# A fused retention and MLP kernel on one core: stores of short units as one stepped transfer, new constants in the emission planner, another order of loads and delays

## The chip, the cores and the metric

The kernel runs on one NeuronCore of a Trainium2 chip. The metric is the device time of one execution in microseconds; less is better. The core has TensorE (PE; its weight loads are shown apart as PEld), VectorE (DVE), ScalarE (ACT), GpSimd (POOL) and SyncE (SP), which run side by side and wait for each other by semaphores, and 16 DMA engines that all transfers share.

## The reference

Causal retention over 8 batches, 8 heads, 576 positions and a head size of 64, and behind it an MLP with an exact GELU:

```
scores = (q @ k^T) / sqrt(64)
gamma  = 1 - 2 ** (-5 - head)
ret    = scores * where(i >= j, gamma ** (i - j), 0)
x      = (ret @ v), heads side by side      # 4608 tokens x 512
out    = gelu_exact(x @ w_in) @ w_out       # 512 -> 2048 -> 512, float32
```

## The kernel before

**Units and blocks.** A batch of 576 positions is cut into chunks of 128; the last one has 64 (TAIL). A *unit* is one chunk of one batch, or, for the tails, the tails of two neighbouring batches together: 64 rows of one and 64 rows of the other, 128 partitions. These are the *short units* (the third entry of their tuple in `units` is None). There are 36 units. Four units make a *block* of 512 tokens for the MLP, nine blocks t = 0 to 8. Units 16 and 17 are short and open block 4; units 34 and 35 are short and are the last two of block 8, the last block.

**Retention.** Per unit or pair of units: loads of q, k and v (POOL's queue, L328, with a cast to bf16), a transpose of q and k (on TensorE for the first groups, L568, by a DMA transpose on SP's queue for the others, L578), scores (L602, L611, L621), the mask on DVE, the inner product with v (L684, L692, L710), the running state (L520, L729) and its product with q (L765). Most of these matmuls are 64 x 64 and use a part of TensorE's array; they are set as groups of 16 to 128 between the MLP's full matmuls.

**MLP.** w_in is applied by L812 (blocks 0 to 5) or by a seven-product Strassen scheme, L1079 (blocks 6 to 8); w_out by L857 (block 0) or by a seven-product scheme, L998. The products of the latter are called M1 to M7 and come in the order M3, M4, M5, M1, M2, M6, M7. For the last two units of a block (tile `hi`), M2 gives the left 256 columns of the output (a copy, L547), M6 the right 256 (L948); for the first two (tile `lo`), M5 and M7 do the same (L958 or L963). In the last block a result is stored as soon as it is there, in pieces.

**The order of the work.** The program is written out straight, without loops on the chip. A planner in the Python code (`fire`, `mlp_pick`, `cand`, the main loop at the end) keeps estimated times of each engine in `T`, of each transfer in two modelled queues (`transfer`, `run_queues`, the costs `MOVE`, the delays SW_LATE and HW_LATE) and of the fetching of TensorE's instructions (`fetch_of`: a block is used up after each 127.7 matmuls, the first after 95; BEGIN, BRING and USE are the times that a fetch takes). It always emits next what it thinks can begin first. Where `stall` says that a group of small matmuls would run into a block not yet fetched by more than STALL, the group is put off. So a changed constant changes no instruction, but which one comes when. `ORDER` is a list found by search: first the order of the loads on POOL's queue (`wi3` is a piece of w_in, `k4` the keys of unit 4, `io` the iota and what hangs on it, `dq2` a decay factor), then entries such as `s10+0.5`, `b24+0.5`, `z12+2.5`, `p29+34`, `u1+8` with delays for scores, inner products, DVE, MLP pieces and haste, and `a17`, units whose v is scaled on ACT instead of DVE.

**Stores.** `store` (L837) writes rows of a unit. A short unit's rows go to two batches; `rows_of` gives the two places, and `store` issues one transfer for each. SP's queue carries the stores and the DMA transposes, in the order of emission; a few stores of the last block go on ACT's queue. At the end of the last block, `after` (L927) does this behind M2 and M6:

```
if last and p == M2:                      # L972
    for x in range(2):
        if units[4 * t + 2 + x][2] is not None:
            store(t, 2 + x, hi[:, x, LEFT], 0, 256)
...
if last:                                  # behind M6, L950
    lo_col = 0 if units[4 * t + 2 + x][2] is None else 256
    store(t, 2 + x, hi[:, x, lo_col:], lo_col, 512, nc.scalar, nc.sync)
```

Both of these units are short, so nothing leaves after M2, and after M6 each unit leaves as two transfers of 64 rows by 512 columns, one on ACT's queue and one on SP's.

Of the kernel before, what the change touches and what calls it, by code (L numbers as in the profile page):

```python
# [17 lines left out]
def kernel(  # L18
# [14 lines left out]
    nc = tc.nc  # L33
    ctx.enter_context(tc.manual_schedule())

    B, H, S, D = q.shape
    d_model = H * D
# [4 lines left out]
    C = 128  # L42
# [5 lines left out]
    TAIL = S - (NCI - 1) * C  # L48
# [5 lines left out]
    units = [(bp, 0, j) for bp in range(2) for j in range(2)]  # L54
# [52 lines left out]
    T = dict.fromkeys(("pe", "act", "dve", "pool", "sp"), 0.0)  # L107
# [9 lines left out]
    for n, keys in enumerate(HW_FIRST):  # L117
        t = o_pool.tile([128, 2, H, D], FP32, tag=f"o{n}", name="first")
        for x, (what, i) in enumerate(keys):
            first[what, i] = t[:, x]  # L120
            src = {"q": q, "k": k, "v": v}[what][2 * units[i][0] + units[i][2]]
# [82 lines left out]
        nc.vector.tensor_tensor(s[:, 3:5], w[:, :, 0:256], w[:, :, 256:512], op=ALU.add)  # L204
        ws_at[i] = on("dve", 1.05, land_out[i]) + SEM

    SW_LATE, HW_LATE = 4.2, 2.8
    TURN_SHARES, STORE_SHARES = (0.455, 0.545), (0.455, 0.545)
    MOVE = {"wi": 1.33, "wo": 1.42, "ld": 0.89, "short": 0.44, "turn": 1.88, "store": 0.9}
    queues = ([], [])  # L210
    moved = [0.0, [0, 0], [None, None]]

# [49 lines left out]
    def sw_dma(issue, kind, put):  # L262
# [3 lines left out]
        T["pool"] += issue  # L266
        flying.append(transfer(0, at, MOVE[kind], put))

    def hw_dma(issue, work, ready, put=lambda end: None, shares=TURN_SHARES):
        at = max(T["sp"], ready)  # L270
        if len(hw_flying) >= 3:
            T["sp"] = max(T["sp"], hw_flying[-3]["end"])
        T["sp"] = max(T["sp"], at + issue)
        hw_flying.append(transfer(1, at, work, put, shares))

    def putter(where, key):
        def put(end):
            where[key] = end
        return put
# [55 lines left out]
    for x, keys in enumerate(zip(*HW_FIRST)):  # L335
        for n, (what, i) in enumerate(keys):
            land[what, i] = (4.6, 5.2)[n] + 0.75 * x
            t = tiles_of(i)
            cast_due[what, i] = (t[1] if what == "v" else t[0][:, "qk".index(what)], first[what, i])
    ORDER = ("wi0 k1 v2 io wi1 q1 v0 k2 v1 q2 wi2 k3 wi3 wi4 q3 wi6 wi5 wi7 v3 k4 wo0 q4 k5 q5 v5 v4 wo1 wo2 dq2 wo3 "  # L340
             "q6 wo4 k7 wo6 q7 dq3 dq0 k6 wo7 v6 v7 wo5 dq4 z12+2.5 p29+34 a17 a31 s10+0.5 z35+2 a30 a23 b24+0.5 s24+4 "
             "s17+0 p25+30 z32+0.2 a13 s12+4 a10 s35+5 s31+5 a27 s18+3 a24 s7+3 u1+8 b25+1.5 a8 p21+36 p27+28 p26+34 "
             "b4+0.8 z27+2 a9 a11 z23+0.2 a25 a26 a5 z4+2.5 b32+4 p35+28 p28+28 a21 b22+3 a15 b17+2 b35+0.5 p30+34 "
             "z16+0.4 z20+1.2 z13+0.8 s14+5 s28+1.5 b30+4 b28+0.5 b8+0.3 s32+5 s29+0.5 z11+0.6 b23+0.5 b12+1.5 p22+30 "
             "b7+4 z34+0.2 s19+5 p20+32 s5+2 z18+0.6 u4+0 b21+0.8 z14+1.2 z26+0.6 b19+0.3 b13+3 s30+1 b20+1 p32+30 "
             "s16+3 b11+4 z33+0.2 b26+0.8 u6+12 z10+0.2 z6+2.5 b5+2 a16 s21+3 z22+0.6 b27+3 z28+2.5 p31+34 u7+12 "
             "b16+1.5 z19+1.2 u3+20 s13+3 s26+5 b9+2 s23+3 s4+1 b33+0.5 z29+0.2 b14+1.5 b18+0.3 z5+1.5 a14 b10+1.5 "
             "b34+0.5 u2+28 s25+0.5 z25+1.5 s34+5 s15+4 s6+3").split()

    BY_ACT = {int(x[1:]) for x in ORDER if x[0] == "a"}  # L350
    S_LATE = {int(x[1:].split("+")[0]): float(x.split("+")[1]) for x in ORDER if x[0] == "s"}
    B_LATE = {int(x[1:].split("+")[0]): float(x.split("+")[1]) for x in ORDER if x[0] == "b"}
    DVE_LAG, P_WAIT, HURRY = ({int(x[1:].split("+")[0]): float(x.split("+")[1]) for x in ORDER if x[0] == kind} for kind in "zpu")
    ORDER = [x for x in ORDER if x[0] not in "abszpu"]

    rest = const.tile([128, 2], BF16, name="rest")

    for n, g in enumerate(groups):
        ORDER += [what + str(i) for what in "qkv" for i in g if what + str(i) not in ORDER and (what, i) not in first]

# [73 lines left out]
    SEM = 0.12  # L434

    CHUNK, FIRST_CHUNK, ASKED = 127.7, 95.0, 150.0
    BEGIN, BEGIN_IDLE, BRING, USE = 4.8, 1.4, 1.2, 1.5
    fetched = {"count": N_WARM, "next": FIRST_CHUNK, "ask": FIRST_CHUNK + CHUNK - ASKED, "ready": [0.0], "landed": 0.0}

    def fetch_of(f, now, dur, n):  # L440
# [133 lines left out]
    def turn_dma(n, jj):  # L574
# [9 lines left out]

        hw_dma(1.3, MOVE["turn"] * (0.62 if short else 1.0), max(land["qk"[jj], i] for i in groups[n]), put)

# [244 lines left out]
    def rows_of(t, ts):  # L831
        bp, ci, j = units[t * 4 + ts]
        if j is not None:
            return [((2 * bp + j) * S + ci * C, 0, C)]
        return [((2 * bp + jj) * S + ci * C, TAIL * jj, TAIL) for jj in range(2)]

    def store(t, ts, src, lo=0, hi=d_model, *on_queues):  # L837
        for x, (row, p0, n) in enumerate(rows_of(t, ts)):
            queue = on_queues[x] if on_queues else nc.sync
            queue.dma_start(out[row:row + n, lo:hi], src[p0:p0 + n])  # L840
        for _ in rows_of(t, ts):
            hw_dma(0.4, MOVE["store"] * (hi - lo) / d_model / len(rows_of(t, ts)), max(T["act"], T["dve"]), putter(o_free, (t, ts // 2)), STORE_SHARES)

    def o_tile(t, x):
        if t == N_BLK - 2:
# [31 lines left out]
    o_free = {}  # L877
# [3 lines left out]
    LEFT, RIGHT = slice(0, 256), slice(256, 512)  # L881
# [45 lines left out]
    def after(t, p, done, piece):  # L927
        lo, hi = o_tiles[t, 0], o_tiles[t, 1]
        last = t == N_BLK - 1
        b, m = held_bank[t, bank_of[p], piece if last and p == M7 else 0]  # L930
        if p == M3:
            nc.scalar.copy(hi[:, :, RIGHT], m)
            at = on("act", 0.6, max(done, o_at(t, 1)))
        elif p == M4:
            for n, (xs, c0, c1) in enumerate(pieces(t)):
                z = held_bank[t, "Z", n] = seeded([128, xs.stop - xs.start, c1 - c0], "m")
                nc.vector.tensor_tensor(z[1], hi[:, xs, 256 + c0:256 + c1], m[:, xs, c0:c1], op=ALU.add)
                at = on("dve", 0.15 + 0.00104 * (xs.stop - xs.start) * (c1 - c0), max(done, read_at[t, M3]))
        elif p == M1:
            v = held_bank[t, "V", 0] = seeded([128, 2, 256], "m")  # L940
            for n, (xs, c0, c1) in enumerate(pieces(t)):
                at = either(0.42 if last else 0.68, done, v[1][:, xs, c0:c1], held_bank[t, "Z", n][1], -1.0)
        elif p in (M5, M2):
            at = either(0.68, max(done, o_at(t, p == M2)), lo[:, :, RIGHT] if p == M5 else hi[:, :, LEFT], m)
            release(b, at + SEM)
        elif p == M6:
            for x in (1, 0) if last else (slice(0, 2),):
                nc.vector.scalar_tensor_tensor(hi[:, x, RIGHT], m[:, x], -1.0, hi[:, x, LEFT], op0=ALU.mult, op1=MINUS)  # L948
                at = on("dve", 0.42 if last else 0.68, max(done, read_at[t, M2]))
                if last:  # L950
                    lo_col = 0 if units[4 * t + 2 + x][2] is None else 256
                    store(t, 2 + x, hi[:, x, lo_col:], lo_col, 512, nc.scalar, nc.sync)
            release(b, at + SEM)
            for x in range(2 * (not last)):
                store(t, 2 + x, hi[:, x, :])
        elif last:
            x, c0, c1 = PIECES[piece]
            nc.vector.tensor_tensor(lo[:, x, c0:c1], m[:, 0], lo[:, x, 256 + c0:256 + c1], op=MINUS)  # L958
            at = on("dve", 0.15 + 0.00104 * (c1 - c0), done)
            release(b, at + SEM)  # L960
            store(t, x, lo[:, x, c0:c1], c0, c1, nc.scalar if piece == 1 else nc.sync)
        else:
            nc.vector.tensor_tensor(lo[:, :, LEFT], m, lo[:, :, RIGHT], op=MINUS)  # L963
            at = on("dve", 0.68, max(done, read_at[t, M5]))
            release(b, at + SEM)
            for x in range(2):
                for c0, c1 in ((0, 256), (256, 512)) if t == N_BLK - 2 else ((0, 512),):
                    store(t, x, lo[:, x, c0:c1], c0, c1)
        if last and p == M5:
            for x in range(2):  # L970
                store(t, x, lo[:, x, RIGHT], 256, 512)
        if last and p == M2:  # L972
            for x in range(2):
                if units[4 * t + 2 + x][2] is not None:
                    store(t, 2 + x, hi[:, x, LEFT], 0, 256)
        read_at[t, p] = at + SEM

    def pieces(t):
# [323 lines left out]
        pe(0.2158 * n, n)  # L1302
        release(b, T["pe"])

    STALL = 0.05

    rest_of = []
    AFTER = [(0.437, 4)] * 6
# [58 lines left out]
    b, t = bank([128, 512], FP32, "warm")  # L1367
# [4 lines left out]
    while True:  # L1372
# [22 lines left out]
        if nA < N_U and not rest_of:  # L1395
            n = group_of[nA]
# [3 lines left out]
        if nB < nA and not rest_of:  # L1400
# [5 lines left out]
            n = group_of[back[0]]  # L1406
# [9 lines left out]
            if not hurry and first:  # L1416
                kind, t = first[0], first[1]
                hurry = nB < 4 * t + 4 if kind in "14" else len(runs[0]) <= HURRY.get(t, 8 if t + 1 >= FAST else 16) and nB < 4 * t + 8 + 4 * (t + 1 >= FAST)
            if hurry:
                n = out_banks(back) + starts(back) + 2 * bool(g)  # L1420
                along = not early and nA >= 4 and scored <= now and len(frees(n)) == n and free_time(n) <= now + 0.3
                cand(ready, "S", g if along else [], back)
        if g and scored < 1e8:
            if early or stuck:
                cand(max(scored, free_time(2)) if nA - nB <= 2 else 1e9, "S", g, [])
            else:
# [4 lines left out]
                if free and (not back or back_at <= now + 0.3) and nA + len(g) <= ahead:  # L1431
                    n = 2 + out_banks(back) + starts(back)
# [13 lines left out]
        if due:  # L1446
            _, kind, a = due[0]
            if kind == "X":
                n = group_of[nX]
# [75 lines left out]
```

## Time and profile before

| | |
|---|---|
| median of 3 runs | 288.71 us (288.49 to 289.89) |
| the profiled execution, its own time | 288.38 us |
| its span, first to last instruction | 286.5 us, TensorE's granted clock 0.998 |
| busy: PE, DVE, ACT, POOL | 276.8, 194.1, 161.2, 115.2 us |
| last arithmetic ends | 281.41 us after the span's start |

The profile shows one execution. Times in it are counted from the span's start. A line of the timeline has start, duration, engine, source line, operation, output and inputs, shape and count, and in brackets the time that the engine was idle just before with what ended it ("issue" means that nothing in the profile ended it). SPq and ACTq are the queues that issue transfers; the duration is that of the issue, the landing comes later. A DMA view has the busy share of the 16 DMA engines in 40 equal slices of its window, in tenths, and the packets of each queue with the time that they took as a share of 16 engines over the window.

### The profile page before, as it was taken

The page shows a single profiled execution, that of the slowest core. Times are in us where ns is not written, and L with a number is a line of the kernel's source. Part 1 is how long each engine was busy: PE and PEld are TensorE (multiplying, and loading weights), DVE is VectorE, ACT ScalarE, POOL GpSimd, SP SyncE. Part 2 cuts the span into 40 slices and gives each one's busy share as a digit, 9 for nine tenths or more (in the row PEclk, how much of TensorE's full clock was granted, in tenths as well). Part 3 has the DMA queues.
Part 4 walks back from the last instruction along what each step waited for, and adds up shares of the span by engine and source line. Part 5 has one row for each costly group of instructions (what it writes and reads, how often), then busy time and mean ns, then how long its engine had stood idle before and what let it go on. Part 6 is the DMA issues. An engine that isn't in the chain of part 4 may idle for free.

```text
span 286.5 us, 9550 instructions
## 1 busy us (share of the span) xinstructions
PE 276.8 (97%) x4076; PEld 207.1 (72%) x4076; DVE 194.1 (68%) x400; ACT 161.2 (56%) x384; POOL 115.2 (40%) x144
## 2 busy tenths in 40 slices
PE   8999999999999999999999999999999999999992
PEld 3588767587865488548864686468888788888892
DVE  4663788628464694999555914994699978869722
ACT  5567835896377911865668338643566445455320
POOL 8978999963555373428462364200000000000000
PEclk9999999999999999999999999999999999999999
DMA  9999999999999999999999999970040000300223
GB/s 141 169 187 172 189 178 163 154 127 160 191 152 218 139 129 138 237 128 145 142 187 186 120 149 158 210 77 2 2 149 2 2 1 19 132 1 2 102 83 111
DMA packets 152507, 35.49 MB, mean 124 GB/s; under 512 B 141072, under 2 KB 148368, under 8 KB 152464
## 3 DMA queue, kind: packets, MB, share of 16 engines
q0 software_dynamic: 116832, 18.10, 97.0%
q1 hardware_dynamic: 34288, 16.19, 33.5%
q10 hardware_dynamic: 1344, 0.59, 0.8%
q8 instruction: 32, 0.52, 0.8%
q14 instruction: 11, 0.09, 0.2%
HBM read 36.70 MB, written 9.44 MB: 161 GB/s over the span
## 4 chain that ended last, share of the span: by engine, by line
PE 73%; POOL 12%; DMA 9%; DVE 1%; issue 1%; SPq 1%; POOLq 0%; DVEq 0%
PE m L998 34%; PE hT L812 21%; PE f L1079 13%; DMA qkT<-qk_ld 4%; DMA w_in<-in_moe_w_in_dram 3%; POOL qk_ld L328 3%; DMA qk_ld<-in_q_dram 3%; POOL v_ld L328 2%; POOL qk L328 2%; POOL w_in L300 2%; PE o_ps L710 2%; POOL w_out L315 2%; PE o_ps L765 1%; POOL dqT L309 1%; PE sc L621 1%; PE u_ps L520 1%
## 5 line engine op out<-in xcount | busy, mean ns | idle before, releaser
L812 PE MATMUL hT<-xT,w_in 128*128 128x512 bf16 (+2 forms) x600 | 87.8, 303 | 0.3 <-ACT g L821 0.3
L821 ACT ACTIVATE g<-hT 128x512 bf16<-128x512 f32 (+1 forms) x107 | 56.4, 551 | 34.5 <-PE hT L812 33.6
L812 PEld LDWEIGHTS <-w_in 128*128 128x128 bf16 x600 | 50.4, 98 | 31.0 <-DMA w_in<-in_moe_w_in_dram 0.5
L998 PEld LDWEIGHTS <-gs 128*128 128x128 bf16 x656 | 62.2, 98 | 7.3
L998 PE MATMUL m<-w_sum,gs 128*128 128x256 bf16 (+1 forms) x400 | 47.9, 268 | 0.0
L328 POOL DMA_DIRECT2D v_ld<-in_v_dram x40 | 33.7, 849 | 22.4 <-DMA qk_ld<-in_k_dram 18.1
L328 POOL DMA_DIRECT2D qk_ld<-in_q_dram x36 | 30.4, 848 | 22.2 <-PE hT L812 6.6
L328 POOL DMA_DIRECT2D qk_ld<-in_k_dram x36 | 30.3, 846 | 19.8 <-DMA qk_ld<-in_q_dram 18.2
L665 ACT ACTIVATE vh<-v_ld,dv 128x64 bf16<-128x64 bf16 x144 | 35.7, 338 | 0.0
L998 PE MATMUL m<-w_out,gs 128*128 128x256 bf16 x256 | 31.9, 273 | 0.0
L893 DVE TENSOR_TENSOR gs<-g 128x1024 bf16<-128x1024 bf16 x32 | 21.8, 688 | 13.7 <-ACT g L821 13.6
L998 PE MATMUL m<-w_sum,g 128*128 128x256 bf16 x256 | 30.6, 273 | 0.0
L998 PEld LDWEIGHTS <-g 128*128 128x128 bf16 x256 | 24.7, 98 | 3.6
L1104 ACT ACTIVATE g<-f 128x512 bf16<-128x512 f32 x36 | 20.5, 591 | 11.6 <-PE f L1079 10.2
L542 DVE CAST u<-u_ps 128x512 bf16<-128x512 f32 x15 | 10.3, 690 | 19.4 <-PE u_ps L520 19.4
L785 DVE TENSOR_TENSOR xT<-o_ps,dqT 128x512 bf16<-128x512 f32 (+1 forms) x36 | 21.0, 625 | 2.5 <-PE o_ps L765 2.4
L897 DVE TENSOR_TENSOR gs<-g 128x1024 bf16<-128x1024 bf16 x32 | 21.6, 687 | 0.0
L547 ACT COPY o<-m 128x512 f32<-128x512 f32 x14 | 8.2, 586 | 23.4 <-PE m L998 23.4
L636 DVE TENSOR_TENSOR ret<-sc,msk 128x512 bf16<-128x512 f32 x28 | 18.6, 684 | 3.5 <-PE sc L621 3.5
L1079 PEld LDWEIGHTS <-w_in 128*128 128x128 bf16 x192 | 18.8, 98 | 2.2
L1079 PEld LDWEIGHTS <-wi 128*128 128x128 bf16 x144 | 14.0, 98 | 2.5 <-issue 0.7
L857 PE MATMUL oT<-w_out,g 128*128 128x512 bf16 x64 | 15.7, 380 | 0.0
(100 smaller groups left out, 335.5 us busy)
## 6 DMA issues: line engine op xcount, KB each, us to landing
out_dram<-o SPq DMA_DIRECT2D x28, 256.0 KB, 7.3
v_ld<-in_v_dram POOLq DMA_DIRECT2D x32, 128.0 KB, 10.7
qk_ld<-in_k_dram POOLq DMA_DIRECT2D x28, 128.0 KB, 9.9
qk_ld<-in_q_dram POOLq DMA_DIRECT2D x28, 128.0 KB, 10.7
w_in<-in_moe_w_in_dram POOLq DMA_DIRECT2D x8, 256.0 KB, 6.8
w_out<-in_moe_w_out_dram POOLq DMA_DIRECT2D x8, 256.0 KB, 7.6
out_dram<-o SPq DMA_DIRECT2D x13, 128.0 KB, 2.3
qk_ld<-in_q_dram POOLq DMA_DIRECT2D x8, 64.0 KB, 11.2
```

Source lines behind the costliest of these rows:

```text
L328: nc.gpsimd.dma_start(dst, src[2 * bp + jj, :, ci * C:ci * C + n, :].rearrange("h s d -> s h d"))
L636: nc.vector.tensor_tensor(r, t, msk.to_broadcast([128, H, L]), op=ALU.mult)
L665: nc.scalar.activation(vh[:, h, :], loaded[i][1][:, h, :], AF.Copy, scale=dv[:, h, ci:ci + 1])
L785: nc.vector.tensor_tensor(x_of(i)[:, :, n * x:n * x + n], o, dqT[:, :, ci * C:ci * C + n], op=ALU.mult)
L812: nc.tensor.matmul(hT[:, m, :], lhsT=w[:, cc, o:o + 128], rhs=x_tiles[t][:, cc, lo:hi], start=(cc == 0), stop=(cc == N_DM - 1))
L821: nc.scalar.activation(g_of(t, m0 // 2)[:, m0 % 2:m0 % 2 + n, lo:hi], hT, AF.Gelu)
L857: nc.tensor.matmul(oT, lhsT=g_of(t, m // 2)[:, m % 2, cols], rhs=w_out_sb[m // 2][:, m % 2, :], start=(m == 0), stop=(m == N_DF - 1))
L893: nc.vector.tensor_tensor(s.rearrange("p m a b -> p m (a b)"), g[:, :, 0, :], g[:, :, 1, :], op=ALU.add)
L897: nc.vector.tensor_tensor(s, g[:, :, :, LEFT], g[:, :, :, RIGHT], op=MINUS)
L998: nc.tensor.matmul(m[:, 0 if apart else ts, :], lhsT=a, rhs=w[:, c0:c1], start=p in begins and mm == 0 and ts == 0, stop=mm == N_DF // 2 - ...
L1079: nc.tensor.matmul(m[:, y, :], lhsT=a[:, c], rhs=d[:, c], start=p in (P1, P7) and y == 0 and c == 0, stop=c == 1, skip_group_check=True)
L1104: nc.scalar.activation(g[:, :, rows, cols], m, AF.Gelu)
```

## The change

Four things are changed:

1. A short unit is stored by one transfer whose output side has a dimension of 2 (the two batches) ahead of 64 rows. In the program the output side is 2 x 64 x 512 or 2 x 64 x 256, where other stores have 128 x 512 or 128 x 256; the SBUF side is 128 partitions. `rows_of` is not called any more.
2. In the last block, after M2 the left halves of units 34 and 35 are stored; after M6 their right halves, one on ACT's queue and one on SP's.
3. Constants of the planner: HW_LATE, the transposes' time, BEGIN, STALL.
4. `ORDER` is another one; with it the order of nearly everything on TensorE.

```diff
-    SW_LATE, HW_LATE = 4.2, 2.8
+    SW_LATE, HW_LATE = 4.2, 3.5
-    MOVE = {"wi": 1.33, "wo": 1.42, "ld": 0.89, "short": 0.44, "turn": 1.88, "store": 0.9}
+    MOVE = {"wi": 1.33, "wo": 1.42, "ld": 0.89, "short": 0.44, "turn": 2.0, "store": 0.9}
-    ORDER = ("wi0 k1 v2 io wi1 q1 v0 k2 v1 q2 wi2 k3 wi3 wi4 q3 wi6 wi5 wi7 v3 k4 wo0 q4 k5 q5 v5 v4 wo1 wo2 dq2 wo3 "
+    ORDER = ("v0 wi2 q1 k1 wi1 q2 io v2 wi0 k2 v1 q3 wi3 k3 v3 wi4 wi5 k4 v4 dq2 k5 q4 wi6 v5 dq3 q5 wo0 wo1 wi7 wo2 "
...
-    BEGIN, BEGIN_IDLE, BRING, USE = 4.8, 1.4, 1.2, 1.5
+    BEGIN, BEGIN_IDLE, BRING, USE = 5.1, 1.4, 1.2, 1.5
...
-    def store(t, ts, src, lo=0, hi=d_model, *on_queues):
-        for x, (row, p0, n) in enumerate(rows_of(t, ts)):
-            queue = on_queues[x] if on_queues else nc.sync
-            queue.dma_start(out[row:row + n, lo:hi], src[p0:p0 + n])
-        for _ in rows_of(t, ts):
-            hw_dma(0.4, MOVE["store"] * (hi - lo) / d_model / len(rows_of(t, ts)), max(T["act"], T["dve"]), putter(o_free, (t, ts // 2)), STORE_SHARES)
+    def store(t, ts, src, lo=0, hi=d_model, queue=nc.sync):
+        bp, ci, j = units[t * 4 + ts]
+        if j is not None:
+            queue.dma_start(out[(2 * bp + j) * S + ci * C:(2 * bp + j) * S + ci * C + C, lo:hi], src)
+        else:
+            rows = out[2 * bp * S:2 * bp * S + 2 * S].rearrange("(b s) d -> b s d", s=S)
+            queue.dma_start(rows[:, ci * C:ci * C + TAIL, lo:hi], src)
+        hw_dma(0.4, MOVE["store"] * (hi - lo) / d_model, max(T["act"], T["dve"]), putter(o_free, (t, ts // 2)), STORE_SHARES)
...
-                    lo_col = 0 if units[4 * t + 2 + x][2] is None else 256
-                    store(t, 2 + x, hi[:, x, lo_col:], lo_col, 512, nc.scalar, nc.sync)
+                    store(t, 2 + x, hi[:, x, RIGHT], 256, 512, nc.scalar if x else nc.sync)
...
-                if units[4 * t + 2 + x][2] is not None:
-                    store(t, 2 + x, hi[:, x, LEFT], 0, 256)
+                store(t, 2 + x, hi[:, x, LEFT], 0, 256)
...
-    STALL = 0.05
+    STALL = 0.2
```

## The prediction

> **What bounds the kernel now.** I read the page first, then the timeline of TensorE, then the last ten microseconds on all engines, then the DMA views of chosen windows.
>
> ```profile
> span 286.5 us, 9550 instructions
> ...
> PE 276.8 (97%) x4076; PEld 207.1 (72%) x4076; DVE 194.1 (68%) x400; ACT 161.2 (56%) x384; POOL 115.2 (40%) x144
> ...
> PE   8999999999999999999999999999999999999992
> ...
> q8 instruction: 32, 0.52, 0.8%
> ```
>
> TensorE has no slack to give away: it is at 9 in 38 of 40 slices. The time is its list of matmuls, plus the few waits inside it, plus what follows its last matmul. The instruction queue matters because it feeds TensorE: 32 packets for 4076 matmuls is one 16 KB block for every 127 or so. These are the long waits (idle time and releaser in brackets; two at "issue", two at DMA, two at ACT or DVE; a seventh, 0.28 us at 10.66, is of the same DMA kind):
>
> ```profile
> 19.48 1.05 PE L812 MATMUL hT<-xT,w_in 128*128 128x256 bf16 x8 [0.30 <-ACT g L821]
> ...
> 43.23 0.73 PE L568 MATMUL qk_ps<-ident,qk_ld 128*128 128x128 bf16 x8 [0.24 <-ACT g L821]
> ...
> 66.17 0.45 PE L621 MATMUL sc<-qkT 64*64 64x64 bf16 x32 [0.52 <-DMA qkT<-qk_ld]
> ...
> 82.66 0.22 PE L765 MATMUL o_ps<-qkT,u 64*64 64x64 bf16 x4 [0.70 <-issue]
> ...
> 161.61 0.42 PE L765 MATMUL o_ps<-qkT,u 64*64 64x64 bf16 x29 [0.56 <-issue]
> ...
> 225.31 0.60 PE L1079 MATMUL f<-xs,wi 128*128 128x256 bf16 x4 [0.52 <-DVE f L1094]
> ```
>
> The other place is the end, here from 277.4 us on:
>
> ```profile
> 277.61 0.59 ACT L547 COPY o<-m 128x512 f32<-128x512 f32 x1 [1.05 <-PE m L998]
> 279.41 0.76 DVE L948 SCALAR_TENSOR_TENSOR o<-m,o 128x256 f32<-128x256 f32 x2 [2.52 <-PE m L998]
> 279.86 2.26 SPq L840 DMA_DIRECT2D out_dram<-o  x4
> 279.87 2.05 ACTq L840 DMA_DIRECT2D out_dram<-o  x3
> ...
> 281.12 0.29 DVE L958 TENSOR_TENSOR o<-m,o 128x128 f32<-128x128 f32 x1 [0.15 <-PE m L998]
> ```
>
> The last arithmetic ends at 281.41, the span at 286.5: five microseconds are stores and their landing. Seven stores go out in 2.3 us. The DMA views of 279.5 to 285 us (40 slices of 0.1375 us) and of 275.4 to 276.6 us (two stores of 128 rows by 1 KB, alone on the engines) say what a store costs:
>
> ```profile
> DMA  0000000000279995999986769699985432210000
> ...
> DMA packets 752, 0.79 MB, mean 143 GB/s; under 512 B 112, under 2 KB 496, under 8 KB 752
> ```
> ```profile
> DMA packets 288, 0.26 MB, mean 219 GB/s; under 512 B 32, under 2 KB 288, under 8 KB 288
> ...
> q1 hardware_dynamic: 288, 0.26, 66.2%
> ```
>
> The first shows packets until slice 36, that is 284.45. In the second, 32 small packets are 16 closing packets for each of two stores: each ran on all 16 engines. 66.2% of 16 engines over 1.2 us is 12.7 engine-us; less 0.3 for the small ones, over 256 packets, **48.5 ns for a 1 KB row**. So such a store takes 128 x 48.5 ns = 6.2 engine-us: 0.39 us on 16 engines, 3.1 us on two. The seven stores of the end have 112 = 7 x 16 closing packets, the four of 64 rows among them.
>
> **The change part by part.** *Planner constants and the new order.* The constants cost nothing themselves; they and ORDER change what the program emits, and I count that in the two lists of instructions. Columns through TensorE are the same. Of 64-wide groups set between 128-wide matmuls there were 38, now 35. One pair of changes costs 0.09 us in (four 109 ns matmuls from 64.54, the next at 65.07) and 0.12 us out, so 3 x 0.21 = -0.63 us. Warm-up matmuls are 37 instead of 35: +0.43 us at 216 ns. hT has 584 matmuls instead of 600 for the same columns: nothing. The iota now stands behind six POOL loads instead of three (2.3 us at 0.7 to 0.9 each); 22 warm-ups instead of 10 stand before the first transpose, 2.6 us, which cover it.
>
> *Fetch waits.* Both "issue" waits come where blocks end by the planner's count (95 + 127.7 k matmuls: 1244 and 2521). What matters is how long the 150 matmuls before such a place last. With group times from the trace (0.38 us for 32 alone, 0.51 for 48, 0.83 for 80, 1.28 for 128) the 150 before 1244 take 7.1 us now and 6.8 changed, before 2521 10.6 and 10.9. So +0.3 at one and as much less at the other: 0, between -1.3 (both gone) and +1.5 (another place as tight as the first: 2266 has 7.9).
>
> *Data waits.* The other five cost 1.9 us of idle time, with the drained pipeline some 2.7. The planner now expects transposes later (2.0 instead of 1.88 us, 0.7 us more delay), which is against the one at 66.17. Which waits the new order brings the list does not tell: -0.3, between -2.7 (all gone) and +2.7 (as many again). TensorE's part: -0.63 + 0.43 + 0 - 0.3 = **-0.5 us**.
>
> *Stores of short units.* The last block's units 34 and 35 are short. Before, after M6, each left as two row halves of 64 x 512 (four issues). Now the left half columns leave after M2 and the right ones after M6, each as one 2 x 64 x 256 store: three on SP, one on ACT, 512 KB as before, each store 128 rows of 1 KB. SP issues one fewer after M6 (0.54 us). Nothing waits on SP behind the M2 stores, it had been idle from 275.5 to 279.86. The unknown is how many engines share such a store. Ends: 16 engines, as every row has it, or two. In this trace every transfer leads with 128 or 64 rows, and its 16 shares are whole leading rows, 8 or 4 each; no row shows a leading row cut in pieces. The new store leads with a count of 2. The nearest rows thus hold under either reading, sharing by packets (16) or by leading rows (2); I take **two**, as whole leading rows are what all have in common, and the same two each time, since one store differs from the next in nothing but its address.
>
> Then the end is: M2's copy is done at 278.20, the issue at 278.25; first packets come 0.8 us after an issue (issue at 242.38, first packets at 243.2), so 279.05. Four stores x 3.1 us = 12.4 us one after the other on the same two engines: 291.45. Behind them M7's three stores with their sixteenths, 8 rows x 48.5 ns and twice 8 half rows x 25 ns, 0.8 us: 292.25, against 284.45. **+7.8 us**. From 281.4 on no engine computes, so nothing hides it.
>
> The Trainium skill, DMA: Bandwidth & Descriptors, section "Why a DMA increments its semaphore by 16 and not by 1", has a rule for this: the engine count is the largest number up to 16 that divides the slowest dimension other than 1 of both sides, and for SP and ACT these are the lowest-numbered engines. By that rule the stores with 128 and 64 rows get 16 (the trace agrees, 16 closing packets each), the new ones two, always the same two, and the sum would be the one above; no run here shows a count under 16.
>
> *The same in block 4* (units 16 and 17, four 64 x 512 stores at 176.48 to 178.99, now two of 2 x 64 x 512). At 88 ns for a 2 KB row (70.8% of 16 engines over 243 to 245 us, 256 rows) two engines are held 2 x 5.6 = 11.3 us, with these behind them:
>
> ```profile
> v_ld<-in_v_dram POOLq DMA_DIRECT2D x2, 64.0 KB, 9.8
> qkT<-qk_ld SPq DMA_TRANSPOSE x5, 5.6
> ```
>
> The last transposes are issued at 189.95 and land at about 195.6; scores of the last pair start at 208.85. 13 us of cover against 11.3: I cost it at 0.
>
> Sum on the profiled execution, 288.38 (span 286.5 and 1.9 around it): 288.38 - 0.5 + 7.8 = **295.7 us**. The median shown, 288.71, lies 0.3 above that execution, well inside the range.
>
> **The rivals.** *All 16 engines share the stepped store.* For it: every store row so far. Against it: none of them led with 2. Then the end gets shorter: 256 KB less in the last rush, and SP's last issue moves from 281.71 to about 281.46. It now lands after 3.2 us; 1.7 is the least of all stores. That is -0.25 to -1.75, I take -0.9: 288.4 - 0.5 - 0.9 = 287.0 us, faster. The point: four stores are 24.8 engine-us, and 279.05 + 24.8 / n + 0.8 = 284.45 at n = 5.4. With six engines or more the end is no later than before.
>
> *16 engines, and TensorE's waits grow*: the 1.5 and 2.7 above, 288.4 - 0.2 + 2.7 - 0.9 = 290.0 at the data bound. For it: the 6.8 us before 1244 and POOL's new order. Against it: the later times that the planner now assumes.
>
> *Two engines, and block 4's stores make the transposes late*: if loads take turns with the stores on these engines, 11.3 us become 20 and the scores at 208.85 wait some 7 us; TensorE has other matmuls to fill part of that: 299 to 303 us. Against it: loads are nearly over at 180.
>
> **How the numbers follow.** Two engines 0.64 (own range 293.0 to 298.4, the bounds of the data waits; those of the fetch waits are not added, since both ends at once are unlikely), 16 engines 0.27 (285.5 to 289.0), 16 with more waits 0.04, two with late transposes 0.05. The range 286.2 to 298.4 reaches over the first two and the third and leaves out the last and the low fifth of the second. 0.5%, about what a measurement here can tell from no change, is 1.4 us: below 287.3 lies a little over half of the second case, 0.15; within it 0.12; slower the rest, 0.73.
>
> **What would show it.** Two engines: 2 instead of 16 closing packets for a stepped store; a last stretch of some 8 us at about an eighth of the DMA share; the last SP wait for a DMA near 10 us instead of 2.4; TensorE's last matmul still near 280. Sixteen: the span ends about 5 us after the last matmul or sooner. TensorE: a wait near matmul 1244 at "issue" of about 1 us; 35 groups; the wait at the first scores with DMA-turned operands gone. The forecast is wrong if the store is shared by packets, or if the stores fall on different pairs of engines, which would bring the end back to about 284.5.

## The result, and the profile after

| | before | after |
|---|---|---|
| median | 288.91 us (288.41 to 291.14, 6 runs) | 301.88 us (301.34 to 306.44, 6 runs) |
| ratio of the times | | 1.0433, 95% interval 1.0393 to 1.0474 |
| profiled execution, its span | 288.38, 286.5 us | 301.66, 299.9 us |
| TensorE's last matmul starts | 280.87 us | 285.92 us |
| last data packet | 284.45 us | 297.85 us |
| closing packets of the last stores | 112 | 56 |

The execution of 306.44 us was in a slower state and is left out of the ratio. The change costs 13 us, where I forecast 7. The time is lost in two places: between 196 and 206 us, and at the end. From the page of the changed kernel (40 slices of 7.5 us):

```profile
span 299.9 us, 9481 instructions
...
PE   8999999999999999999999999959999999999910
...
PEclk9999999999999999999999999977999999999995
DMA  9999999999999999999999999290120003002221
```

TensorE's row has a 5 in the slice from 195 to 202.4 us, where the row of before had 9, and its granted clock a 7 there and in the next. Its last two slices are nearly empty. TensorE's timeline, waits in brackets:

```profile
83.04 0.39 PE L997 MATMUL m<-w_sum,gs 128*128 128x256 bf16 x2 [0.56 <-issue]
...
196.12 0.60 PE L1078 MATMUL f<-xT,w_in 128*128 128x256 bf16 x4
198.97 1.66 PE L997 MATMUL m<-w_sum,gs 128*128 128x256 bf16 x8 [2.25 <-issue]
201.40 1.01 PE L1078 MATMUL f<-xs,wi 128*128 128x256 bf16 x4 [0.77 <-DVE f L1093]
```

Two stops stand close together, 2.25 us of idle time at "issue" and 0.77 us at VectorE. Eight matmuls take 1.66 us at 198.97, where 8 of this form take 1.03 to 1.04 elsewhere. Against run 1 below, which has the same order and no stop here, TensorE's weight loads are 0.1 us ahead up to 196.3 us and 6.1 us behind from 206.9 us on: it lost 6.2 us.

The last stores, on all queues (start, duration; SPq and ACTq rows are issues):

```profile
283.28 2.49 SPq L842 DMA_DIRECT2D out_dram<-o  x3
...
285.87 5.86 SPq L839 DMA_DIRECT2D out_dram<-o  x2
```

and the DMA view from 284 to 300 us (40 slices of 0.4 us):

```profile
DMA  0111110126422111147425221111111100000000
...
DMA packets 953, 0.79 MB, mean 50 GB/s; under 512 B 56, under 2 KB 952, under 8 KB 952
```

Long stretches stand at 1, where two busy engines of 16 would be 0.125. Of the 56 small packets, 48 are the 16 of each of M7's three plain stores; the four stepped stores have 8 together, two each. Two engines it was.

### The profile page after: what moved, and what is told of

Read it like the earlier page. It is cut to its first block, busy times and chain, and to the rows that moved or that the text cites. A ratio compares the mean times of both kernels' runs of the same rounds, so it can differ in the third digit from the quotient of the medians.

```text
span 299.9 us, 9481 instructions
## 1 busy us (share of the span) xinstructions
PE 279.9 (93%) x4062; PEld 207.1 (69%) x4062; DVE 191.8 (64%) x399; ACT 157.5 (53%) x357; POOL 114.9 (38%) x144
## 4 chain that ended last, share of the span: by engine, by line
PE 86%; DVE 4%; DMA 2%; issue 2%; POOL 1%; ACT 0%; DVEq 0%; POOLq 0%
PE m L997 32%; PE hT L811 28%; PE f L1078 11%; PE oT L858 4%; DMA qk<-in_k_dram 2%; PE o_ps L709 2%; PE sc L620 2%; PE u_ps L519 1%; PE qk_ps L567 1%; PE o_ps L764 1%; PE warm L1300 1%; DVE f L1093 1%; DVE xT L784 1%; DVE gs L894 1%; DVE gs L898 1%
## 5 line engine op out<-in xcount | busy, mean ns | idle before, releaser
L811 PE MATMUL hT<-xT,w_in 128*128 128x512 bf16 (+3 forms) x584 | 87.3, 306 | 0.1
L820 ACT ACTIVATE g<-hT 128x512 bf16<-128x512 f32 (+2 forms) x107 | 57.7, 552 | 35.4 <-PE hT L811 34.7
L811 PEld LDWEIGHTS <-w_in 128*128 128x128 bf16 x584 | 49.4, 98 | 32.2 <-DVE xT L784 0.5
L997 PEld LDWEIGHTS <-gs 128*128 128x128 bf16 x656 | 63.0, 99 | 11.5 <-issue 3.3
L997 PE MATMUL m<-w_sum,gs 128*128 128x256 bf16 (+1 forms) x400 | 49.2, 271 | 2.8 <-issue 2.8
L997 PE MATMUL m<-w_out,gs 128*128 128x256 bf16 x256 | 33.3, 278 | 0.0
L664 ACT ACTIVATE vh<-v_ld,dv 128x64 bf16<-128x64 bf16 x112 | 28.0, 337 | 0.1
L1103 ACT ACTIVATE g<-f 128x512 bf16<-128x512 f32 x36 | 20.3, 589 | 10.1 <-PE f L1078 9.4
L546 ACT COPY o<-m 128x512 f32<-128x512 f32 x15 | 8.8, 586 | 25.6 <-PE m L997 22.4
L1078 PEld LDWEIGHTS <-w_in 128*128 128x128 bf16 x192 | 18.9, 99 | 2.8 <-issue 0.3
L541 DVE CAST u<-u_ps 128x512 bf16<-128x512 f32 x13 | 8.9, 688 | 14.8 <-PE u_ps L519 14.6
L667 DVE TENSOR_TENSOR vh<-v_ld,dv 128x512 bf16<-128x512 bf16 x22 | 14.8, 684 | 3.4 <-DMA v_ld<-in_v_dram 3.3
```

Source lines behind the costliest of these rows:

```text
L664: nc.scalar.activation(vh[:, h, :], loaded[i][1][:, h, :], AF.Copy, scale=dv[:, h, ci:ci + 1])
L667: nc.vector.tensor_tensor(vh, loaded[i][1], dv[:, :, ci:ci + 1].to_broadcast([128, H, D]), op=ALU.mult)
L811: nc.tensor.matmul(hT[:, m, :], lhsT=w[:, cc, o:o + 128], rhs=x_tiles[t][:, cc, lo:hi], start=(cc == 0), stop=(cc == N_DM - 1))
L820: nc.scalar.activation(g_of(t, m0 // 2)[:, m0 % 2:m0 % 2 + n, lo:hi], hT, AF.Gelu)
L997: nc.tensor.matmul(m[:, 0 if apart else ts, :], lhsT=a, rhs=w[:, c0:c1], start=p in begins and mm == 0 and ts == 0, stop=mm == N_DF // 2 - ...
L1078: nc.tensor.matmul(m[:, y, :], lhsT=a[:, c], rhs=d[:, c], start=p in (P1, P7) and y == 0 and c == 0, stop=c == 1, skip_group_check=True)
```

## The experiments

Except for the last one, every kernel here has the instruction order of the kernel that it is made from, on TensorE, VectorE, ScalarE and GpSimd; only transfers differ. They are made from the changed kernel; the fourth is made from the kernel before. The theory: the stepped stores stand on two engines, which makes the end long, and in block 4 they hold up what else these engines carry, TensorE's next instruction block and the transposes among it. The rival for the stop: the new order makes it.

**1. The changed kernel with halves.**

```diff
-            queue.dma_start(rows[:, ci * C:ci * C + TAIL, lo:hi], src)
+            for jj in range(2):
+                queue.dma_start(rows[jj, ci * C:ci * C + TAIL, lo:hi], src[TAIL * jj:TAIL * jj + TAIL])
```

> The changed kernel, but each stepped store of a short unit is issued as two stores of 64 rows, in the same place and on the same queue; instructions on TensorE, VectorE, ScalarE and GpSimd stand in the same order as in the changed kernel. Theory (stepped stores run on two engines, and block 4's two of them also cause the stop of TensorE at 196 us by holding up its instruction block and the DMA transposes): no stop at 196, last matmul at about 279.7 instead of 285.9, the end 5 us or less behind it, 286.8 us. Rival (the stop at 196 comes from the new order of the work, only the long end from the stores): stop and half-speed matmuls stay, last matmul near 285.9, about 292 us.

Measured: 288.52 us, ratio to before 0.9966, interval 0.9929 to 1.0003, so no difference from before is shown. The stop and the half clock are gone, the last stores have 176 closing packets, 11 times 16, and the last matmul starts at 279.82. The whole loss hangs on the form of these six transfers. The 286.8 was 1.7 us too low: I had put the span's end at 5 us or less behind the last matmul, and it came 6.6 us behind (5.7 in before). The last packet comes 4.36 us after the last matmul instead of before's 3.58, with eleven issues there instead of seven.

**2 and 3. Each place alone.** In the second run block 4 is stored in halves and the last block stepped, as here; in the third, with 8 in place of 4, the reverse.

```diff
-            queue.dma_start(rows[:, ci * C:ci * C + TAIL, lo:hi], src)
+            if t == 4:
+                for jj in range(2):
+                    queue.dma_start(rows[jj, ci * C:ci * C + TAIL, lo:hi], src[TAIL * jj:TAIL * jj + TAIL])
+            else:
+                queue.dma_start(rows[:, ci * C:ci * C + TAIL, lo:hi], src)
```

> The changed kernel with block 4's short units stored as row halves of 64 rows; the last block's four stores stay stepped. Theory: TensorE as in e1_halves (no stop at 196), the end 13 us behind the last matmul as in the changed kernel: 301.7 - 6.3 = 295.4 us. Rival (order makes the stop): 301.7 us, nothing changes.

> The changed kernel with the last block's short units stored as row halves; block 4's two stores stay stepped. Theory: the stop at 196 and the half-speed stretch stay, the end is short: 301.7 - 8.8 = 292.9 us. A rival in which block 4's stores do not matter gives the time of e1_halves.

Measured: 294.83 and 291.79 us (one execution each). With only the last block stepped there is no stop, the last matmul starts at 279.10, and the last packet follows it by 11.94 us (4.36 with halves): +7.6 us is the price of the end. With only block 4 stepped the end is short (3.72 us), and TensorE stops. Its timeline in the third kernel:

```profile
198.31 1.03 PE L1001 MATMUL m<-w_sum,gs 128*128 128x256 bf16 x8 [1.95 <-issue]
200.52 0.67 PE L1082 MATMUL f<-xs,wi 128*128 128x256 bf16 x4 [1.18 <-DVE f L1097]
```

The same two stops, and half clock for 3.41 us from 200.91 on: 1.95 + 1.18 + 3.41 / 2 = 4.8 us, and its last matmul starts 4.65 us later than with halves. So block 4 costs that much here. In the changed kernel the half clock lasts 6.83 us, which costs another 1.7 us. The time alone would not show it, since the slowest execution with halves took 291.26 us; the trace does.

**4. The kernel before with stepped stores**, its order and constants kept: units 34 and 35 still leave behind M6 alone, now as one 2 x 64 x 512 transfer each.

> The kernel before, order and constants untouched, with each short unit stored by one stepped transfer of 2 x 64 x 512 (block 4's two on SP, the last block's after M6, one on ACT and one on SP). Theory: at the end two stores of 64 rows of 2 KB on each of two engines, 11.3 us from 281.0 and M7's shares, so 293.1 instead of 284.45, and a late instruction block or late transposes after block 4's stores here too: 288.4 + 8.6 + 0 to 6 = 297 to 303 us. Rival (order makes the stop): 297.0 us with TensorE as before.

Measured: 302.81 us (one execution). The stop is there without the new order, so the rival falls:

```profile
201.32 0.81 PE L1002 MATMUL m<-w_sum,gs 128*128 128x256 bf16 x6 [3.32 <-issue]
```

TensorE's instruction packet began at 189.76 and took 10.1 us; all the others of these nine full kernels took 0.9 to 1.9 us. The last 2 KB packet of the stepped stores ended at 197.81. The order is another one, and still this stop has 3030 of TensorE's weight loads ahead of it, as the stop at "issue" has in the changed kernel and in run 3: the end of an instruction block by the prediction's count, 95 + 127.7 x 23 = 3032. But behind this stop, the longest of all, the clock stayed at full speed. Run 8 says why.

**5. The new order with the old way of storing**: the changed kernel with `store` and the two places in `after` as before.

```diff
-                    store(t, 2 + x, hi[:, x, RIGHT], 256, 512, nc.scalar if x else nc.sync)
+                    lo_col = 0 if units[4 * t + 2 + x][2] is None else 256
+                    store(t, 2 + x, hi[:, x, lo_col:], lo_col, 512, nc.scalar, nc.sync)
...
-                store(t, 2 + x, hi[:, x, LEFT], 0, 256)
+                if units[4 * t + 2 + x][2] is not None:
+                    store(t, 2 + x, hi[:, x, LEFT], 0, 256)
```

> The changed kernel's order of loads and delays and its model constants, with the store code of the kernel before: each short unit as two 64-row pieces, the last block's four pieces of 64 x 512 after M6's pass on ScalarE's and SyncE's queues, none after M2's. With halves at the changed kernel's places TensorE ended 1.05 us earlier than before (279.82 against 280.87) and the time stood 0.3 us under before, because its end took about 0.7 us longer. My theory, that the new order gains about 1 us on TensorE and the old way of storing has the shorter end: 287.5 to 288 us, 0.3 to 0.5% under before, no stop near 196 us. Rival, that the gain on TensorE belongs to this or that placing of the transfers and not to the order: 288.7 to 289.2, no difference.

Measured: 287.57 us, ratio 0.9953, interval 0.9924 to 0.9981. It is the one version below the kernel before by more than its interval, by 0.2 to 0.8%. The last matmul starts at 280.20, the last packet comes 3.38 us later.

**6 and 7. What decides the number of engines.** Plain row pieces, cut at 62 of 64 rows as here, then with 48 in place of 62; nothing steps over the batches.

```diff
-            queue.dma_start(rows[:, ci * C:ci * C + TAIL, lo:hi], src)
+            for jj in range(2):
+                for a, z in ((0, 62), (62, TAIL)):
+                    queue.dma_start(out[(2 * bp + jj) * S + ci * C + a:(2 * bp + jj) * S + ci * C + z, lo:hi], src[TAIL * jj + a:TAIL * jj + z])
```

> The changed kernel with every short unit stored as four plain row pieces, 62 and 2 rows of each half, in the place of the stepped transfer; nothing steps over the two batch rows. Theory (a transfer's rows go to as many engines as the largest number up to 16 that divides its outer count: 62 gives 2): the last block and block 4 again stand on two engines each, so TensorE stops near 196 us and the end is as long as the changed kernel's, 300 to 305 us, with 2 closing packets for each piece. Rival (it is the list that steps over two batch rows that is slow, and 62 plain rows are spread over 16 engines): as the 48 and 16 cut, 288 to 291 us, no stop.

> The same four pieces for each short unit, of 48 and 16 rows, both of which 16 divides. Theory: 16 closing packets for each piece, no stop near 196 us, 288 to 291 us: the time with halves (288.5) and up to 2 us for twice as many issues at the end. Rival (it is the number of issues and of pieces that costs, not the number of engines): as slow as the 62 and 2 cut, whatever that gives.

Measured: 298.43 us (297.17 and 299.68, two runs) and 289.44 us (ratio 0.9978 to 1.0048 of before). The last stores have 80 closing packets with 62 and 2 rows, 48 of M7's stores and two for each of 16 pieces, and 304 with 48 and 16, sixteen for each piece. The windows are 277 to 286 us of run 1, 279 to 294.5 of run 6 and 277 to 290 of run 7:

```profile
DMA packets 1073, 0.80 MB, mean 89 GB/s; under 512 B 176, under 2 KB 1072, under 8 KB 1072
```
```profile
DMA packets 977, 0.80 MB, mean 52 GB/s; under 512 B 80, under 2 KB 976, under 8 KB 976
```
```profile
DMA packets 1202, 0.81 MB, mean 62 GB/s; under 512 B 304, under 2 KB 1200, under 8 KB 1200
```

The last packet follows the last matmul by 11.46 and by 5.28 us. So the long end needs no step, since 62 plain rows go to two engines as well, and the number of issues does not make it. The Trainium skill, DMA: Bandwidth & Descriptors, section "Why a DMA increments its semaphore by 16 and not by 1", says that the engines are as many as the largest number up to 16 that divides the slowest dimension other than 1 of both sides. The counts 64, 62, 48, 16 and 2 agree (16, 2, 16, 16 and 2 closing packets). Which two engines they are, no run here shows.

I had expected 300 to 305 us with 62 rows. The miss is in block 4. In the profiled execution the instruction packet was through at 196.21 instead of 197.33 and ScalarE's copy to p (below) started at 198.27 instead of 200.03; no stop at "issue" came, only the one at VectorE, and no half clock:

```profile
199.63 0.60 PE L1080 MATMUL f<-xs,wi 128*128 128x256 bf16 x4 [0.90 <-DVE f L1095]
```

So waits that ended one or two microseconds earlier cost 5 us less. The other execution took 2.5 us longer and has no trace, so whether the stop came there is not known.

**8. The clock by itself.** Nothing of the reference is computed. The part of the kernel that matters:

```
for again in range(4):
    for level in range(14):
        columns = 1000 + 200 * level
        while columns > 0:
            n = min(columns, 400)
            nc.vector.tensor_copy(seen[:, :n], t[:, :n])
            columns -= n
        x += 1
        matmuls(90 + 7 * x % 17)
```

> Nothing of the reference is computed: TensorE runs 90 to 106 matmuls of 512 columns of zeros between stops, and each stop waits for VectorE's copies of 1000 to 3600 PSUM columns (some 1.2 to 4.2 us), 56 stops in all; the output is a constant. In the seven profiles so far the granted clock changed only on a grid of 3.413 us (194.56 us and 279.89 us are 57 and 82 of them), fell to 0.5 after a grid window in which TensorE stood for 1.99 us or more (1.99, 2.25, 2.28) and kept 1.0 after 1.92 or less (1.92, 1.82, 1.56). Theory, that the share of one window decides: stops under 1.9 us never lower the clock, stops of 2.0 to 3.9 us lower it only where more than about 1.95 us falls within one window, stops above 3.9 us always, and half speed lasts whole windows. Rival, that the length of a stop decides, wherever it lies: one length from which every stop lowers the clock. Rival two, that two stops close together are needed: no single stop below 3.4 us lowers it.

Measured: in each record the clock changes on one grid of 3.413 us. It fell to half after every grid window in which TensorE stood for 2.09 us or more, and kept its speed after every one with 2.06 us or less. It rose again after windows with 0.68 us or less and stayed at half after those with 1.05 or more. I had expected the bound at about 1.95. By their length the 56 stops say less: all 32 of 3.50 us or more lowered the clock, none of 1.89 us or less did, and of the four stops at each length of 2.3, 2.5, 2.9 and 3.1 us some did and some did not. Three stops of 2.28 to 2.29 us, cut along the grid. A row has the window and its length, the busy time and count of PE, PEld, DVE (in the full kernels also ACT) and POOL, then the granted clock, the DMA share and GB/s:

```profile
69.00:72.41 3.41, 1.12 (x6) 0.39 (x4) 2.09 (x4) 0.00 (x0) 1.00 0.00 0
72.41:75.83 3.42, 3.42 (x10) 1.20 (x9) 0.00 (x0) 0.00 (x0) 0.50 0.00 0
437.64:441.05 3.41, 1.60 (x8) 0.61 (x7) 1.71 (x3) 0.00 (x0) 1.00 0.00 0
441.05:444.46 3.41, 2.94 (x14) 1.36 (x14) 0.38 (x2) 0.00 (x0) 1.00 0.00 0
806.27:809.69 3.42, 1.82 (x9) 0.71 (x8) 1.49 (x3) 0.00 (x0) 1.00 0.00 0
809.69:813.10 3.41, 2.72 (x13) 1.26 (x13) 0.60 (x2) 0.00 (x0) 1.00 0.00 0
```

The first stop lies within one window (busy 1.12, so 2.29 idle), and the next window runs at 0.50. The other two fall on a border, and nothing happens. So the length does not decide, nor does it take two stops: the share of one window does. Read with that, the fourth kernel's stop:

```profile
195.99:199.40 3.41, 2.01 (x19) 1.66 (x17) 0.70 (x1) 0.59 (x1) 0.00 (x0) 1.00 1.06 62
199.40:202.82 3.42, 1.50 (x14) 1.34 (x14) 0.14 (x1) 0.59 (x1) 0.00 (x0) 1.00 0.53 86
```

It is split 1.40 to 1.92 and stays under the bound. The changed kernel's windows:

```profile
195.80:199.22 3.42, 1.17 (x12) 0.90 (x10) 0.00 (x0) 0.00 (x0) 0.00 (x0) 1.00 1.51 84
199.22:202.63 3.41, 2.64 (x14) 1.68 (x12) 0.88 (x2) 1.58 (x3) 0.00 (x0) 0.50 0.38 73
202.63:206.04 3.41, 3.41 (x17) 2.35 (x16) 0.51 (x1) 1.29 (x3) 0.00 (x0) 0.50 0.00 0
```

The first stop fills 2.25 us of its window: half clock. The second, in the next window, leaves 0.77 us idle there, and the clock did not rise; so a second window is run at half speed.

## Why the prediction failed, by its steps

**Block 4's stores: "I cost it at 0".** This is the step that failed. That they run on two engines and hold them for long was right; who waits for these engines was not, and "long" was put too short. I had looked for the wait at one place, the scores at 208.85. The DMA view from 174 to 196 us (0.55 us a slice) after, and with halves:

```profile
DMA  9999999999999999999999111111111111112999
```
```profile
DMA  9999981999899999999919089201058009600000
```

The view counts a packet in the slice in which it starts. From 186 to 193 us the packets that started kept two engines busy. Some others were under way but did not end: 17 packets of the transposes, 256 B each, began between 184.8 and 186.0 and ended at 194.3 to 194.4. The stepped stores' 256 packets ran from 180.2 to 194.1, 13.9 us instead of 11.3. From 186 to 194 us 146 of them stand beside 152 load packets of 128 B: on these engines stores and loads took turns, as the last rival had it. SyncE's queue after (start, duration):

```profile
174.39 3.43 SPq L842 DMA_DIRECT2D out_dram<-o  x2
177.94 20.46 SPq L577 DMA_TRANSPOSE qkT<-qk_ld  x5
```

The row runs from the first of the five transposes' issues to the end of the last. The first issue alone took 12.24 us of it, with halves 1.43. Three things were late by the stores, as the waits from 186 to 206 us show (total, times, longest):

```profile
DVE f L1093 <- PE m L997: 5.4, 1, 5.4
ACT p L546 <- DMA qkT<-qk_ld: 4.9, 1, 4.9
ACT o L546 <- DMA out_dram<-o: 3.3, 1, 3.3
PEld L997 <- issue: 2.4, 1, 2.4
```

ScalarE's copy to o waited 3.3 us for the stepped store itself. With halves it waits 2.91 us there too, for TensorE, so it was only some 0.4 us late. Its next copy, p, waited 4.9 us for the transposes; with halves it ran at 195.12, now at 200.03. It does not read their result. The program takes p's tile from the same ring of five buffers (`tag="qk"`, L1087) as the `qk_ld` tiles that the transposes read, so it needs the room which they free. In before this copy ran at 196.51, 12 us ahead of the scores that I had given as cover. VectorE's sum f waits for p and TensorE for the sum, 0.77 us; the view names PE m in VectorE's wait, as what came last by the profile, and in run 3 it names ACT p. The third is TensorE's instruction block. With halves its packet started at 189.06, here at 195.50, when the two engines had come to the end of the stores (last 2 KB packet 193.98), and "issue" is the 2.25 us. That the packet came late because of the stores follows from runs 1 and 3; why it set out only at 195.50, where run 4's set out at 189.76 and took 10.1 us, is not shown. I had named that queue as the one that feeds TensorE, and then left it out of the list of what stands behind the stores.

The price: idle 2.25 + 0.77, and (6.83 - 0.77) / 2 = 3.03 by the half clock, 6.05 of the 6.2 us. The two stops do not simply add. VectorE's sum ends at 201.35 whether the block is late or not. With the block in time, by my estimate from these rows, TensorE would have run its eight matmuls to 197.60 and then stood 3.8 us for the sum. Of these, 2.2 us would lie in the window from 199.22 on, enough for one window at half clock: some 5.5 us instead of 6.05. So the late transposes alone would have cost most of the price. In run 4 it is the late block alone that stops TensorE. That a stop of some 2 us halves the clock behind it was in no term of the sum. The rival "two engines + late transposes", with 0.05, gave 299 to 303, which holds the time, but by luck: it had the scores waiting, not the instruction block and the copy to p, and nothing of the clock. Its chance was too low because "loads are nearly over at 180" was read from before's trace, where nothing held the loads up, and spoke of one kind of traffic alone.

**The end: right.** Forecast +7.8 us, measured +8.35 in the profiles (last packet less last matmul: 11.93 against 3.58) and +7.6 between the first two experiments. The 1 KB packets of the end ran from 284.45 to 297.68, 13.2 us; 12.4 + 0.8 was forecast. The first of them came 1.2 us behind its issue, not 0.8. That the stores share the same two engines was right too: the view above stands at 0 or 1 up to 287.2 us, with the four stepped stores issued between 283.28 and 285.25. The sign "last SP wait near 10" came in two parts: SP's issue behind the stepped stores took 4.24 us for the first of M7's two pieces, and then this, in SP's waits:

```profile
SPq L1519 <- DMA out_dram<-o: 6.2, 1, 6.2
```

**TensorE's part, -0.5 us: right in direction, half the size.** The last matmul of the four kernels with the new order and no stop between 190 and 206 us (runs 1, 2, 5, 7) starts 0.3 to 1.8 us earlier than before's, 0.95 in the mean. The idle times over 0.15 us add up to 3.1 us in before and to 1.9 to 2.8 in these four, 1.0 less in the mean, where I had -0.3 for the waits; the -0.63 and +0.43 for groups and warm-ups can't be told beside that. Each of these is one execution, and a wait changes from one to the next: the one at "issue" near matmul 1244 is 0.70 us in before and 1.74 in run 4, whose list is the same up to there. In the changed kernel it is 0.56 (I had said about 1), with the same order it is 0.50 in run 6, 0.91 in run 7 and under 0.15 in runs 1, 2, 3 and 5. So the sum came out near, and no run shows its terms one by one. The wait at the first scores with DMA-turned operands is gone, as forecast. In the prediction's list of six waits the brackets name a DMA once and ScalarE or VectorE three times, not two and two; the sum does not depend on it.

**The rivals with 16 engines** are refuted by the closing packets. Whether a stepped store on 16 engines would end 0.9 us sooner stays open, since none ran so; the nearest, run 1, with the left halves stored after M2 by all 16, ended 0.8 us later behind the last matmul than before (4.36 against 3.58).

"TensorE's last matmul still near 280" was the sign that would have told the failed step: it came at 285.92.

## What to carry to other kernels

Write a transfer so that its outermost count on both sides has 16 as a divisor; the closing packets in the DMA view show how many engines it got, and an issue saved is worth far less than fourteen idle engines (run 7 has 12 issues more than run 1 and takes 0.9 us more by the medians, 1.4 by the ratios to before). To cost a transfer that fills few engines, list everything else that these engines carry in that time, loads, transposes and TensorE's instruction blocks, and for each the first instruction that waits for it or for the room that it frees. Where several are late, the wait that ends last decides. A stop of TensorE has to be priced with the clock window in which it lies.

## What the runs showed of the hardware

- The clock gate looks at windows of 3.413 us on a fixed grid: 194.56 and 279.89 us at full speed are 57 and 82 of them. Idle time between 2.06 and 2.09 us within one window was the bound in run 8; in the full kernels 1.92 kept the clock and 1.99 did not (ends of matmuls are modelled, so the two need not agree to 0.1 us). The longest stop that left the clock alone was 3.32 us, 3.10 in run 8. The Trainium skill, TensorE: Matmul & The Clock Gate, section "Part 1: The HAM clock gate (the "warmup" mystery)", has a free-running window of 3413 ns and half speed after at least one idle window. The length agrees with the 3.413 us here; of a window, 2.09 us idle (61%) was enough here, and the measurement decides.
- A 16 KB instruction packet, 0.9 to 1.9 us everywhere else, took 10.1 us in run 4; block 4's stepped stores were under way for the first 8 of these.
- Stores of block 4 on two engines did not always stop TensorE at "issue": in run 6's profiled execution, with the rows cut at 62, its instruction packet ended 1.1 us earlier than in the changed kernel, and this stop did not come.
